# Linear attention followed by a channel mix on one core: a new order table with new engine and PSUM choices

## The chip, the cores and the metric

The kernel runs on one core of one Trainium2 chip. The metric is the device time of one execution in microseconds (us); less is better. The engines that appear below are TensorE (PE, with its weight loads PEld), VectorE (DVE), ScalarE (ACT), GpSimd (POOL) and SyncE (SP, which here only issues transfers). Every engine works through its own instructions in order and waits for others by semaphores. PSUM is the memory into which TensorE writes its results.

## The reference

Two layers follow each other. The first is linear attention over 8 batches, 8 heads, 576 positions and head size 64, the second a channel mix over the 512 joined channels. Cut to what is computed:

```python
def phi(x):                                   # w_phi is 64 x 128
    proj = np.einsum('bhsd,df->bhsf', x, w_phi)
    proj = proj - np.max(np.abs(proj), axis=-1, keepdims=True)
    return np.concatenate([np.exp(proj), np.exp(-proj)], axis=-1)
q_p, k_p = phi(q), phi(k)
kv = np.einsum('bhsf,bhsd->bhfd', k_p, v)
z = np.sum(k_p, axis=2)
attn = np.einsum('bhsf,bhfd->bhsd', q_p, kv) / (np.einsum('bhsf,bhf->bhs', q_p, z)[..., None] + 1e-06)
x = attn.transpose(0, 2, 1, 3).reshape(8, 576, 512)
x_prev = x moved down by one position, zero in front
xk = mu_k * x + (1.0 - mu_k) * x_prev
xr = mu_r * x + (1.0 - mu_r) * x_prev
k = np.maximum(xk @ w_k, 0.0)                 # w_k is 512 x 1024
v = k * k @ w_v                               # w_v is 1024 x 512
out = v / (1.0 + np.exp(-(xr @ w_r)))         # w_r is 512 x 512
```

Inputs and output are float32; the kernel multiplies in bfloat16.

## The kernel before

The attention is cut into 32 pairs of heads, pair n being heads 2a and 2a+1 of batch b with n = 4b + a. The channel mix is cut into 8 batches, and two neighbouring batches share one more tile of 128 positions, the edge tile `e0` to `e3`. Every piece of work is an `op` with a name, an engine and a function that issues its instructions. The names, with the line of `kernel.py` that their instructions carry in the profile:

For the pairs (number n behind the name): `pt` transposes k and q on TensorE (L338), `pa` and `pb` copy the two halves of it out of PSUM; from batch 2 on `tr` does the same by a transposing transfer on SP's queue (L352). `kp` and `qp` project k and q (L566), `rk` and `rq` take the maxima (VectorE reductions, L579 and L584), `em` and `ea`, `eb` are the exponentials for k on ScalarE (L591, L605), `va` and `vb` scale v by a factor from `em` (L597). `mh`, `mt`, `mc` bring the maxima of q into the layout that `qt`, the projection of q in transposed form, adds (L615, L620, L630); `qa` and `qb` are the exponentials for q (L643). `kv` multiplies k's features with v (L656), `kc` copies the product, `nd` forms numerator and denominator (L677), `ra` and `rd` divide (L685, L689). Then the result is transposed: for pairs 0 to 7 by `xt` on TensorE and the copies `xe`, `xf` (L715), for the others by the transposing transfer `xz` on SP's queue (L700) and the small copy `xu` (L706). `df` is the difference to the position before (L726), and `xa` and `xb` mix with `mu_k` and `mu_r` (VectorE, L732).

The last 64 positions of the pairs of one batch are done together by small operations whose names carry the batch: `tp`, `rt`, `mhe`, `mte`, `mce`, `eme`, `ekt`, `qte`, `eqe` (batch 0 has three such groups, `0.0`, `0.1`, `0.2`).

For the channel mix (batch and part behind the name): `h` multiplies with `w_k` (eight parts, L810), `rl` is the rectification (L206 on ScalarE, L208 on VectorE), `sq` the square (L212 on ScalarE, L214 on VectorE or GpSimd), `r` multiplies with `w_r` (four parts, L829), `th` is a hyperbolic tangent that gives the sigmoid (L835), `v` multiplies with `w_v` (four parts, L843), `ob` joins them (VectorE, L849) and `so` stores on SP's queue (L856). `rle`, `sqe`, `he`, `re`, `ve` belong to the edge tiles.

Loads: `hk` and `hq` bring the first pair in float32, `lk0.0.d` and `lq0.0.d` cast it; `lk` and `lq` load k and q of a batch (GpSimd's queue, L321), `lv` loads v (two halves `.0` and `.2` of each batch; GpSimd's or SP's queue, L327), `wk`, `wr`, `wv` the weights in two parts each (GpSimd's queue, L432). A load issued by GpSimd stands in the same order as its computations.

No loop decides the order. One string, `ORDER`, lists all 1498 names, and the kernel calls them in that order; what an engine executes is that list with the other engines' entries left out. Behind a name stand the choices: `/ENG` is the engine where there is one to choose, `:i` the PSUM tile, `+n@i` are n matmuls on constants ahead of the operation, into tile i, that keep TensorE busy. Entries that end in `.d`, and `tr0` to `tr31`, issue nothing, except the two casts.

```python
    def order(self):
        self.place = {}
        out = []
        for word in ORDER.split():
            name, _, n = word.partition("+")
            name, _, on = name.partition("/")
            name, _, i = name.partition(":")
            out.append(self.ops[name])
            out[-1]["on"] = on
            out[-1]["fill"] = tuple(map(int, n.split("@"))) if n else None
            for (tag, key) in out[-1]["alloc"]:
                if tag in ("P", "mo"):
                    self.place[key] = int(i)
```

PSUM has two tiles of one bank, M0 and M1, for `pt`, `xt`, `mt`, `mte`, `qte` and all channel-mix products, and three of two banks, P0 to P2, for the projections (`tp` among them), `qt`, `kv` and `nd`. An operation that takes a tile waits until its last reader is done. Buffers in SBUF are few as well, and a later use waits for the earlier one: `BUFS` gives 2 for k's features (`kpn`), for q's (`qpn`) and for the differences `d`, 3 for the rectified parts (`krelu`) and for v (`vt`), 4 for the outputs (`ob`).

The code that issues the work is the same before and after; the functions that the change reaches through the table follow.

Of the kernel before, what the change touches and what calls it, by code (L numbers as in the profile page):

```python
# [31 lines left out]
eb3 pt6.1:0 pt7.0:1 va2/POOL pb6/DVE tr6 qt2:2 pa7/ACT ra1 rd1 mte0.2:0 qa2 lk2.0 lk2.0.d pt7.1:1
mce0.2/DVE qp5:0 pb7/DVE tr7 qte0.2:0 lq2.0 lq2.0.d qb2 rq5 tp1.0:1 xt0:1 va3/POOL eqe0.2 kv2:2
rt1.0 xf0/ACT xe0/ACT kp4:0 mh4/POOL mt3:0 kc2/ACT rk4 xt1:1 df0/POOL mc3/ACT ekt1.0 nd2:2 ra2 ea4
vb3/POOL xe1/DVE qt3:1+1@0 rd2 mt4:0 xf1/ACT mc4/ACT df1/DVE qa3 xt2:1 xa0 kv3:2 eb4 mhe1.0/DVE
xe2/DVE mte1.0:0+1@0 xb0 kc3/ACT kp5:0 qb3 qt4:2 xa1 eme1.0 xf2/DVE nd3:1 rk5 mce1.0/ACT df2/POOL
qa4 ra3 qb4 rd3 lv1.2/POOL lv1.2.d ea5 xa2 xt3:0+7@1 qp6:2 xb1 qte1.0:1 xe3/ACT qp7:1 eb5 xf3/DVE
df3/DVE xa3 em4 qt5:0+1@0 eqe1.0 rq6 vb4/POOL h0.0:0 qa5 va4/POOL rq7 kp6:2 qb5 h0.1:1 rk6 mh6/POOL
kp7:1 rl0.1/ACT kv4:0 va5/POOL rl0.0/ACT tr2.0 tr2.0.d tr8 tr9 mt6:1 kc4/DVE ea6 h0.2:0 rk7 vb5/POOL
eb6 xb2 kv5:0+1@2 mc6/ACT sq0.0/ACT xb3 nd4:2 tr2.2 tr2.2.d tr10 tr11 em6 ea7 h0.3:1 kc5/DVE  # L40
vb6/POOL ra4 rd4 nd5:0 eb7 vb7/POOL rl0.3/DVE qt6:2 rl0.2/ACT ra5 qp8:1 rd5 qa6 lv2.0/SP lv2.0.d
sq0.1/POOL r0.0:1 rq8 qb6 va6/POOL qp9:0 h0.4:0 rq9 th0.0 sq0.3/POOL sq0.2/ACT qt7:2 kv6:1 rl0.4/DVE
qa7 lk3.0 lk3.0.d tp2.0:0 kc6/DVE h0.5:1 mh8/POOL rt2.0 qb7 va7/POOL xt4:0 rl0.5/ACT kp8:1 xf4/DVE
# [973 lines left out]
```

## Time and profile before

| what | value |
|---|---|
| runs | 280.14, 289.3, 278.56 us; median 280.14 |
| profiled execution, span | 275.3 us, granted TensorE clock 1.00 in every stretch |
| profiled execution, own time beside the span | not recorded |
| TensorE | 261.7 us busy in 3682 matmuls |
| VectorE | 234.6 us busy in 388 instructions |
| ScalarE | 223.1 us busy in 413 instructions |
| GpSimd | 142.4 us busy in 193 instructions |
| transfers | 42.89 MB in 65817 packets, 156 GB/s over the span |

The span runs from the first to the last record of one execution; the runs' times lie some microseconds above it. "Busy" counts instructions that compute; a transfer's issue is not counted, though it occupies the engine that issues it. In a list of groups the columns are the line, the engine, the operation with output and input, the count, busy time and mean ns of one instruction, then the idle time ahead of the group's instructions and what ended most of it. In a table by stretch each row gives the length of the stretch, the busy time of each engine with the count of instructions, the granted clock, and the share and rate of the transfers.

Times of some operations in this execution, as they are used below: `kp0` starts at 7.01 us, `ea0` at 8.84, the first channel-mix matmul `h0.0` at 39.6, `h1.0` at 78.4, `va12` at 83.0, `h2.0` at 113.4, `h4.0` at 170.8, `h5.0` at 190.6, `va28` at 203.3, `h6.0` at 226.5, `h7.0` at 248.8 and `v7.0` at 258.3; the matmuls end at 271.05 and the last store at 275.3. `lq0.1` is issued at 2.15 and `wk.1` at 12.2.

### The profile page before, as it was taken

What the parts mean: (1) busy time and instruction counts of PE and PEld (TensorE: products, weight loads), DVE (VectorE), ACT (ScalarE), POOL (GpSimd) and SP (SyncE); (2) the same over time, 40 slices, a digit from 0 to 9 for tenths busy, and PEclk for the clock granted to TensorE, in tenths of its full rate; (3) what the DMA queues carried; (4) which work ended last, traced back from release to release, by engine and by line L of the source; (5) the groups of instructions that cost most, each with busy time, mean ns of one, the idle gap of its engine ahead of it and who ended that gap; (6) DMA issues with size and microseconds to landing.
All of it is one profiled execution on the core that took longest, in us unless ns stands there. A gap on an engine that the chain in (4) does not pass through costs nothing.

```text
span 275.3 us, 8865 instructions
## 1 busy us (share of the span) xinstructions
PE 261.7 (95%) x3682; PEld 154.1 (56%) x3730; DVE 234.6 (85%) x388; ACT 223.1 (81%) x413; POOL 142.4 (52%) x193
## 2 busy tenths in 40 slices
PE   7899889999899999999999999999999999999993
PEld 3567656566555566555565666555566565444542
DVE  6999999999799989999999889998889897864222
ACT  3899999999899997899898999789987777616330
POOL 5799557976818682633459465821931611300200
PEclk9999999999999999999999999999999999999999
DMA  7999999599999899759699998981725324142134
GB/s 147 285 209 250 209 213 174 114 235 175 238 129 200 202 219 185 155 127 248 99 166 164 215 249 142 171 255 41 161 89 88 77 52 100 42 110 67 29 88 116
DMA packets 65817, 42.89 MB, mean 156 GB/s; under 512 B 47152, under 2 KB 57008, under 8 KB 65776
## 3 DMA queue, kind: packets, MB, share of 16 engines
q1 hardware_dynamic: 54496, 27.54, 49.3%
q0 software_dynamic: 11056, 14.42, 29.1%
q8 instruction: 29, 0.48, 0.8%
q10 hardware_dynamic: 224, 0.36, 0.5%
q14 instruction: 12, 0.10, 0.1%
HBM read 33.62 MB, written 9.44 MB: 156 GB/s over the span
## 4 chain that ended last, share of the span: by engine, by line
PE 75%; DVE 8%; ACT 6%; issue 4%; DMA 3%; POOL 2%; SPq 0%; POOLq 0%; ACTq 0%
PE ps_h L810 19%; PE ps_v L843 17%; PE ps_r L829 9%; PE ps_nd L677 5%; PE ps_kv L656 5%; DMA qkT<-nat 3%; PE ps_he L897 3%; PE ps_ve L929 3%; PE ps_k L566 2%; PE ps_qT L630 2%; PE ps_q L566 2%; PE ps_qT L636 2%; ACT k L605 2%; DVE nmk L579 2%; PE ps_f L292 1%
## 5 line engine op out<-in xcount | busy, mean ns | idle before, releaser
L597 POOL TENSOR_TENSOR v<-vt,v 128x576 bf16<-128x576 f32 x59 | 69.8, 1203 | 33.5 <-ACT v L591 31.1
L605 ACT ACTIVATE k<-ps_k 128x1024 bf16<-128x1024 f32 x64 | 64.8, 1047 | 1.3 <-DVE nmk L579 1.3
L643 ACT ACTIVATE q<-ps_qT 128x1024 bf16<-128x1024 f32 x64 | 63.8, 1054 | 1.8 <-PE ps_qT L636 1.7
L810 PE MATMUL ps_h<-xk,wk_bf 128*128 128x512 bf16 x235 | 60.5, 380 | 1.2
L843 PE MATMUL ps_v<-wv_bf,kk 128*128 128x512 bf16 x244 | 58.2, 379 | 0.6
L579 DVE TENSOR_REDUCE nmk<-ps_k 128x8 f32<-128x1024 f32 x32 | 38.8, 1217 | 1.8 <-PE ps_k L566 1.5
L584 DVE TENSOR_REDUCE nmq<-ps_q 128x8 f32<-128x1024 f32 x32 | 38.3, 1217 | 1.6 <-PE ps_q L566 1.4
L843 PEld LDWEIGHTS <-kk 128*128 128x128 bf16 x256 | 24.1, 98 | 27.3
L810 PEld LDWEIGHTS <-wk_bf 128*128 128x128 bf16 x256 | 22.7, 97 | 25.0 <-issue 0.7
L206 ACT ACTIVATE krelu<-ps_h 128x512 bf16<-128x512 f32 x48 | 28.8, 611 | 9.3 <-PE ps_h L810 9.3
L726 POOL TENSOR_TENSOR diff<-xs 128x576 bf16<-128x576 bf16 x15 | 20.2, 1346 | 28.8 <-ACT xs L706 12.7
L214 POOL TENSOR_TENSOR kk<-krelu 128x512 bf16<-128x512 bf16 x18 | 19.1, 1068 | 30.3 <-ACT krelu L206 26.6
L849 DVE SCALAR_TENSOR_TENSOR ob<-rt,ps_v 128x512 f32<-128x512 bf16 x32 | 21.7, 682 | 14.3 <-PE ps_v L843 12.7
L829 PE MATMUL ps_r<-wr_bf,xr 128*128 128x512 bf16 x116 | 31.1, 380 | 0.7
L835 ACT ACTIVATE rt<-ps_r 128x512 bf16<-128x512 f32 x32 | 19.7, 615 | 8.8 <-PE ps_r L829 8.7
L732 DVE SCALAR_TENSOR_TENSOR xk<-diff,mu_k_t,xs 128x576 bf16<-128x576 bf16 x32 | 26.7, 839 | 0.1
L689 DVE TENSOR_TENSOR x_sc<-ps_nd,rden 128x640 bf16<-128x640 f32 x32 | 26.0, 817 | 0.6
L732 DVE SCALAR_TENSOR_TENSOR xr<-diff,mu_r_t,xs 128x576 bf16<-128x576 bf16 x32 | 25.6, 806 | 0.1
L656 PE MATMUL ps_kv<-v,k 64*128 64x65 bf16 x1024 | 22.4, 190 | 0.5 <-ACT q L643 0.2
L566 PEld LDWEIGHTS <-qkT 64*128 64x128 bf16 x512 | 16.5, 94 | 11.0 <-issue 8.0
L656 PEld LDWEIGHTS <-k 64*128 64x128 bf16 x1024 | 19.3, 94 | 5.7 <-issue 1.8
L677 PE MATMUL ps_nd<-kv,q 128*128 128x65 bf16 x512 | 21.4, 193 | 0.0
(102 smaller groups left out, 414.3 us busy)
## 6 DMA issues: line engine op xcount, KB each, us to landing
out_dram<-ob SPq DMA_DIRECT2D x70, 128.0 KB, 2.5
vt<-in_v_dram SPq DMA_DIRECT2D x11, 576.0 KB, 6.1
nat<-in_k_dram POOLq DMA_DIRECT2D x6, 576.0 KB, 7.8
nat<-in_q_dram POOLq DMA_DIRECT2D x6, 576.0 KB, 8.0
vt<-in_v_dram POOLq DMA_DIRECT2D x4, 576.0 KB, 6.0
wk_bf<-in_moe_w_k_dram POOLq DMA_DIRECT2D x2, 512.0 KB, 11.4
wv_bf<-in_moe_w_v_dram POOLq DMA_DIRECT2D x2, 512.0 KB, 10.6
nat<-in_k_dram POOLq DMA_DIRECT2D x3, 288.0 KB, 6.9
```

Of the source, the lines that this page charges most:

```text
L206: nc.scalar.activation(out_, in_, AF.Relu, scale=HALF)
L579: nc.vector.tensor_reduce(t[:, j, :], s["k"].rearrange("p a (g f) -> p (a g) f", f=128), axis=AX.X, op=ALU.max, apply_absolute_value=True, ...
L584: nc.vector.tensor_reduce(t[:, j, :], s["q"].rearrange("p a (g f) -> p (a g) f", f=128), axis=AX.X, op=ALU.max, apply_absolute_value=True, ...
L597: (nc.vector if eng == "DVE" else nc.gpsimd).tensor_tensor(vb[:, a, pn, :, 0:64], vt[b, a // 2][:, a % 2, :].rearrange("p (s d) -> p s d", ...
L605: nc.scalar.activation(s[f"k{pn}"], s["k"].rearrange("p a (g f) -> p (a g) f", f=128), AF.Exp, scale=(1.0 if pn == 0 else -1.0))
L643: nc.scalar.activation(t.rearrange("f x (a p) -> f x a p", a=2), s["qT"].rearrange("f a (x p) -> f x a p", p=64), AF.Exp, scale=(1.0 if pn ...
L656: nc.tensor.matmul(ps[:, hh, pn * 65:(pn + 1) * 65], lhsT=s[f"k{pn}"][r, c, :], rhs=vb[r, a, pn, 2 * g + par, :], start=(pn == 0 and c == ...
L677: nc.tensor.matmul(ps[:, bk, o * 65:(o + 1) * 65], lhsT=tail if sl < 2 else s[f"q{pn}"][:, 2 * G + h, :], rhs=s["kv"][:, h, pn, :], start= ...
L732: nc.vector.scalar_tensor_tensor(out=t[:, a, (b % 2) * S:(b % 2 + 1) * S], in0=s["d"], scalar=mu[:, a:a + 1], in1=xs[:, a, 0:S], op0=ALU.m ...
L810: nc.tensor.matmul(ps, lhsT=wk_bf[:, c, fc * 128:(fc + 1) * 128], rhs=xkt[bp][:, c, m0:m0 + 512], start=(c == 0), stop=(c == NDC - 1))
L829: nc.tensor.matmul(ps, lhsT=xrt[bp][:, c, m0 + ci * 128:m0 + (ci + 1) * 128], rhs=wr_bf[:, c, :], start=(c == 0), stop=(c == NDC - 1))
L843: nc.tensor.matmul(ps, lhsT=s["kk"][:, fc, ci * 128:(ci + 1) * 128], rhs=wv_bf[:, fc, :], start=(fc == 0), stop=(fc == NFC - 1))
```

## The change

Only the string `ORDER` is rewritten. The same 1498 names stand in it, with the same matmuls on constants. 148 entries have another engine, 151 another PSUM tile, and a large part stand at another place. The engine choices that differ, by kind (from, to, count):

| kind | changes |
|---|---|
| `sq` | ACT to POOL 14, DVE to POOL 7, DVE to ACT 5, POOL to DVE 4, POOL to ACT 2, ACT to DVE 1 |
| `sqe` | DVE to POOL 4, ACT to DVE 2 |
| `rl`, `rle` | ACT to DVE 13, DVE to ACT 12 |
| `df` | DVE to POOL 9, POOL to DVE 3 |
| `xu` | ACT to POOL 7, ACT to DVE 3, POOL to DVE 2, POOL to ACT 2, DVE to POOL 1 |
| `va`, `vb` | POOL to DVE 6, DVE to POOL 2 |
| `lv` (issue) | SP to POOL 6, POOL to SP 2 |
| `kc` | DVE to ACT 5, ACT to DVE 4 |
| `mc`, `mce` | ACT to DVE 7, DVE to ACT 5 |
| `mh`, `mhe` | DVE to POOL 4, POOL to DVE 4 |
| `pa`, `pb`, `xe`, `xf` | DVE to ACT 6, ACT to DVE 4 |
| casts of the first pair | k: DVE to ACT, q: ACT to DVE |

At the start, `pt1.1` moves ahead of `tp0.0` and `kp0`, and most of GpSimd's load issues stand in one row behind `kp1`. The first part of the table:

```diff
--- before.py
+++ after.py
-ones hk hq ident dve2 hk.d hq.d wphi wphi.d lk0.1 lk0.1.d lq0.1 lq0.1.d mus mus.d lk0.2 lk0.2.d dve3
-lq0.2 lq0.2.d lv0.0/POOL lv0.0.d lk0.0.d/DVE lq0.0.d/ACT lv0.1/SP lv0.1.d pt0.0:0+9@0 lv0.2/SP
-lv0.2.d pt0.1:1 pa0/DVE pb0/ACT tr0 dve1 tp0.0:0+1@2 kp0:1 rt0.0 qp0:2 rk0 eme0.0 mhe0.0/POOL ekt0.0
-pt1.0:1+1@0 lk1.0 lk1.0.d pa1/ACT mte0.0:0 rq0 ea0 lq1.0 lq1.0.d pt1.1:1+2@2 pb1/DVE tr1 lk1.2
-lk1.2.d eb0 kp1:2+2@2 tp0.1:0 lq1.2 lq1.2.d rt0.1 em0 rk1 qp1:1+1@1 ekt0.1 mh0/POOL eme0.1 wk.0
-wk.0.d mt0:1+1@1 mc0/ACT mce0.0/DVE rq1 ea1 qt0:0+1@2 wk.1 wk.1.d wk.d pt2.0:1 qa0 pt2.1:0
...
+hk wphi mus wphi.d mus.d ident lk0.1 lq0.1 lk0.1.d lq0.1.d hq ones dve2 dve3 hk.d hq.d lk0.0.d/ACT
+lq0.0.d/DVE pt0.0:1+9@0 pa0/DVE pt0.1:0 pt1.1:1+2@2 pb0/ACT tr0 dve1 tp0.0:0+1@2 rt0.0 kp0:1
+pt1.0:0+1@0 qp0:2 rk0 pb1/ACT ekt0.0 pa1/ACT eme0.0 ea0 em0 eb0 tr1 rq0 kp1:2+2@2 tp0.1:0 rt0.1
+lk0.2 lq0.2 lk1.0 lv0.1/POOL lq1.0 lk1.2 wk.0 mh0/POOL lq1.2 lv0.0/SP lv0.0.d mhe0.0/POOL vb0/POOL
+lv0.2/POOL lk0.2.d lq0.2.d mt0:1+1@1 pt2.0:0 mc0/ACT qp1:1+1@1 ekt0.1 eme0.1 pa2/ACT qt0:0+1@2
```

Up to the first channel-mix matmul, and into the stretch behind it (`xb0` ahead of `rd2`; `sq0.0` on POOL):

```diff
-eb3 pt6.1:0 pt7.0:1 va2/POOL pb6/DVE tr6 qt2:2 pa7/ACT ra1 rd1 mte0.2:0 qa2 lk2.0 lk2.0.d pt7.1:1
...
-vb3/POOL xe1/DVE qt3:1+1@0 rd2 mt4:0 xf1/ACT mc4/ACT df1/DVE qa3 xt2:1 xa0 kv3:2 eb4 mhe1.0/DVE
-xe2/DVE mte1.0:0+1@0 xb0 kc3/ACT kp5:0 qb3 qt4:2 xa1 eme1.0 xf2/DVE nd3:1 rk5 mce1.0/ACT df2/POOL
...
-eb6 xb2 kv5:0+1@2 mc6/ACT sq0.0/ACT xb3 nd4:2 tr2.2 tr2.2.d tr10 tr11 em6 ea7 h0.3:1 kc5/DVE
-vb6/POOL ra4 rd4 nd5:0 eb7 vb7/POOL rl0.3/DVE qt6:2 rl0.2/ACT ra5 qp8:1 rd5 qa6 lv2.0/SP lv2.0.d
-sq0.1/POOL r0.0:1 rq8 qb6 va6/POOL qp9:0 h0.4:0 rq9 th0.0 sq0.3/POOL sq0.2/ACT qt7:2 kv6:1 rl0.4/DVE
...
-kp9:0 h0.6:1 rk9 lv2.2/POOL lv2.2.d eb8 kv7:2 th0.2 df4/DVE qp11:1 sq0.5/DVE rl0.6/ACT h0.7:0 xa4
...
+ea3 pb5/ACT tr5 pt6.1:1 eb3 pb6/ACT qt2:2 qa2 pt7.1:0 lk2.0 mhe0.2/POOL lq2.0 va2/POOL va3/POOL
+vb2/POOL wk.1 vb3/POOL lv1.0.d qp5:0 mte0.2:1 tr6 mce0.2/ACT pb7/DVE rq5 tr7 wv.1.d wv.0.d wv.d qb2
...
+xt1:1 mt3:0 nd2:2 xf1/ACT mc3/ACT ea4 mt4:0 kv3:1 mc4/ACT kc3/ACT qt3:1+1@0 eb4 xe1/DVE ra2 df0/POOL
+xb0 rd2 wr.0 df1/POOL xa0 xb1 wr.1 xt2:1 kp5:0 qt4:2 lk2.0.d wk.1.d wk.d lq2.0.d qa3 qb3 eme1.0
...
+df2/POOL vb4/POOL va5/POOL vb5/POOL va4/POOL lv1.2/POOL xa2 xe3/DVE xf3/DVE mce1.0/DVE df3/DVE xa3
+qp7:1 qp6:2 qte1.0:1 qt5:0+1@0 rq6 h0.0:0 rq7 wr.1.d wr.0.d wr.d lv1.2.d eqe1.0 qa5 rl0.0/ACT qb5
+kp6:2 h0.1:1 rk6 kv4:1 kc4/DVE xb2 rl0.1/ACT mh6/POOL sq0.0/POOL sq0.1/POOL kv5:0+1@2 ea6 eb6 tr2.0
+tr2.0.d tr8 tr9 kc5/DVE kp7:1 mt6:1 h0.3:0 nd5:0 nd4:2 rk7 rl0.3/ACT ea7 em6 eb7 sq0.3/POOL
+lv2.0/POOL vb6/POOL lk3.0 va6/POOL h0.2:0 rl0.2/ACT tr2.2 tr2.2.d mc6/DVE xb3 ra5 ra4 rd4 rd5 r0.0:1
...
+vb7/POOL sq0.4/POOL lk4.0 mh8/POOL lv2.2/POOL lq3.0.d lv2.0.d rk8 ekt2.0 th0.1 ea8 eme2.0 eb8 r0.2:0
...
+sq0.5/POOL v0.1:0 vb9/POOL va9/POOL df4/POOL mh10/POOL df5/POOL rk11 ob0.1 xb4 xa4 xa5 eqe2.0
...
+xt7:1 tp3.0:0 kv10:2 xt6:0 kp12:1 kc10/ACT xf6/ACT xf7/ACT rt3.0 qt10:2 xe6/DVE rk12 xe7/DVE
+mhe3.0/DVE ekt3.0 r0.3:0 nd9:0 v0.3:1 lk5.0 df6/POOL df7/POOL vb11/POOL xa6 ra9 rd9 xa7 lq4.0.d qa10
```

Behind that, the entries of SP's queue (`xz`, `so`), the loads of v and `va16`:

```diff
-kp12:2 xf7/ACT xf6/DVE qt10:1 xe6/DVE ekt3.0 xz8 xz8.d xe7/DVE r0.3:0 df6/DVE qa10 rk12 df7/POOL
...
-h1.5:1 rk15 sq1.4/POOL eb14 lv4.0/SP lv4.0.d r1.2:0 lk5.0 lk5.0.d xz11 xz11.d rl1.5/DVE ea15 qp16:2
...
-rle0.1/ACT kp16:2 vb14/POOL qp17:0 qa14 so1.0 so1.0.d v1.1:1 rq17 va14/POOL qb14 xz12 xz12.d rk16
...
-xa11 eme4.0 ve0:0 em16 ra15 ob1.3 qa16 va16/POOL so1.2 so1.2.d rd15 qb16 h2.0:1 va17/POOL obe0 xz14
...
-h5.3:1 mh28/POOL sq5.1/ACT lv7.2/POOL lv7.2.d rq30 eme7.0 v4.1:0 kc26/ACT vb27/POOL ea28 rl5.3/DVE
-vb29/DVE rl5.4/ACT xb22 nd27:0 rl5.5/ACT h5.6:1 ra26 eb29 sq5.4/DVE rd26 h5.7:0 df24/DVE xz26 xz26.d
...
+eqe3.0 r1.0:1 rq12 rq13 so0.1 so0.0 so0.2 xz8 lv3.0/SP xz8.d em12 th1.0 r1.1:0 qp14:1 h1.2:1 nd11:0
...
+ob1.0 xz12 xz11 xz11.d so1.0 lv4.2/POOL lq5.0.d ekt4.0 qp17:1 qt14:2 kp16:0 rq17 rk16 so0.0.d xz12.d
...
+mc16/DVE r1.3:1 vb15/POOL df10/POOL lv4.0/POOL va15/POOL sqe0.0/POOL sqe0.1/POOL kc14/ACT ra13 rd13
...
+vb16/POOL vb17/POOL obe0 tr5.0 tr5.2 so1.2 xz13 xz13.d lv5.0/SP so1.3 soe0 xz14 xz15 so1.1 va16/DVE
...
+ra27 mc28/DVE nd26:1 h5.5:0 rd27 sq5.4/DVE ra26 rd26 so4.1 xz25 soe1 xz25.d ea29 em28 vb29/DVE
+rl5.5/ACT eb29 h5.6:1 h5.7:0 va29/POOL so4.2 lv7.2/SP xz27 so4.0 sq5.5/POOL rl5.6/ACT rl5.7/ACT
...
+vb30/DVE ra28 rd28 xa25 mt30:0 kv30:0 mc30/ACT th5.3 kc30/ACT kv31:2 qt30:1 so5.1 xz26 xz26.d
```

`lv5.2` is issued by SP in the old table and by POOL in the new one.

## The prediction

> **What bounds the kernel now.** The page's table of engines comes first. It names no single limit: TensorE is busy nearly all the time, VectorE and ScalarE over four fifths of it, and only GpSimd (POOL) is half idle.
>
> ```profile
> PE 261.7 (95%) x3682; PEld 154.1 (56%) x3730; DVE 234.6 (85%) x388; ACT 223.1 (81%) x413; POOL 142.4 (52%) x193
> ```
>
> An average over 275.3 us hides stages with different limits, so the second view is busy time by stretch. I cut at 39.6 (the first MoE matmul, `h0.0`), 83.0 (`va12`) and 203.0 (`va28`), and 271.0, where the matmuls end.
>
> ```profile
> core 0: us, PE busy (x) PEld busy (x) DVE busy (x) ACT busy (x) POOL busy (x), PEclk, DMA share, GB/s
> 0.00:39.60 39.60, 34.48 (x557) 22.32 (x560) 35.49 (x76) 33.92 (x75) 28.81 (x50) 1.00 1.12 224
> 39.60:83.00 43.40, 41.09 (x737) 25.48 (x746) 41.64 (x66) 41.67 (x74) 30.58 (x36) 1.00 0.99 176
> 83.00:203.00 120.00, 118.53 (x1763) 69.65 (x1787) 111.48 (x168) 109.14 (x200) 70.84 (x95) 1.00 0.89 174
> 203.00:271.00 68.00, 67.58 (x636) 36.63 (x640) 45.55 (x80) 38.34 (x68) 12.13 (x14) 1.00 0.35 76
> ```
>
> Up to 39.6 the vector engines set the pace: TensorE idles 5.1 us. From 39.6 to 83 VectorE and ScalarE are each 96% busy and TensorE still idles 2.3 us. After 83 TensorE is the limit, idle 1.5 us of 120 and 0.4 of 68. So an order can win at most the idle 5.1 + 2.3 + 1.5 + 0.4 = 9.3 us, and it can lose without limit.
>
> The third view, the chain that ended last, agrees: TensorE holds three quarters of it.
>
> ```profile
> PE 75%; DVE 8%; ACT 6%; issue 4%; DMA 3%; POOL 2%; SPq 0%; POOLq 0%; ACTq 0%
> ```
>
> The fourth is the list of POOL's waits. It is idle because it works in order and what it needs is late; two of the entries name the VectorE mixes of line 732.
>
> ```profile
> POOL v L597 <- ACT v L591: 31.1, 11, 9.3
> POOL kk L214 <- ACT krelu L206: 26.6, 4, 15.3
> POOL diff L726 <- DVE xr L732: 5.5, 2, 3.7
> POOL v L597 <- DVE xk L732: 2.2, 1, 2.2
> ```
>
> The fifth is the order of time around 166 us. While VectorE's `xk` runs (166.02 to 166.83), POOL's `diff` takes 1.74 us against 1.28 in most of its runs, about the 0.59 they share.
>
> ```profile
> 166.02 0.81 DVE L732 SCALAR_TENSOR_TENSOR xk<-diff,mu_k_t,xs 128x576 bf16<-128x576 bf16 x1
> 166.24 1.74 POOL L726 TENSOR_TENSOR diff<-xs 128x576 bf16<-128x576 bf16 x1 [2.41 <-PE ps_qT L636]
> ```
>
> Over the whole timeline, 39 of the 64 reductions at lines 579 and 584 lie for more than 60% of their length beside a POOL computation, and 3 of the 64 mixes at line 732 do; the 22 squares on VectorE never do. So VectorE operations with two SBUF inputs (mixes, `df`, `sq`, `va`) and POOL computations take turns, and their times add.
>
> The Trainium skill (SBUF — State Buffer, Who interferes with whom) says the same more strictly: the pair of ports that VectorE and GpSimd share is "an exclusive lock", the loser of the race waits for the whole instruction, and a VectorE operation with two SBUF inputs takes part only against a GpSimd operation that reads SBUF. The row above shows both running for part of the time in the records. By the rule, which lets nothing overlap, the middle stretch below comes to +1.0 at least; by the rows, which leave room for overlap, it may be as low as -1.4. The rule speaks against this change.
>
> **The change part by part.** No operation is added or removed, the warm-up matmuls included. 148 operations and load issues change engine and 151 change PSUM tile. TensorE's own order moves little: before `h0.0`, `h1.0`, `h2.0`, `h4.0`, `h5.0` and `v7.0` stands the same matmul work. So TensorE's 261.7 us stay, and the sum is about its idle time.
>
> *Start, 0 to 39.6.* `pt1.1` (transposes of pair 1) is moved ahead of `tp0.0` and `kp0`. It needs both loads of pair 1; `lq0.1` is issued at 2.15 and the page gives such a load 5.4 us, so it lands at about 7.55. Behind `pt1.1` on TensorE wait `tp0.0` (6.94 now) and `kp0` (7.01), and for these the first reductions and the first exponentials. Four transposes (0.2 to 0.3 us) and two fills later `kp0` starts at about 8.0, 1.0 later. ScalarE also gets `pb1` (0.59) ahead of `ea0`, which goes from 8.84 to about 10.0. From there to the end of `qb3` its queue took 25.6 us without a pause; the new table adds `pa2` 0.69, `mce0.0` and `mce0.2` 0.30 each, `pb6` 0.59, `mc2` 0.28, and takes out `pa7` 0.69 and `xe0` 0.71: +0.8. So `qb3` ends at 10.0 + 25.6 + 0.8 = 36.4 against 34.5. `nd3` follows 0.5 later, `ra3` and `rd3` end at 38.0 (36.8 now), and `xa2`, `xe3`, `xf3`, `mce1.0`, `df3`, `xa3` (0.73 + 0.45 + 0.18 + 0.22 + 0.46 + 0.81) bring `h0.0` to 40.9 at best. VectorE walked in the same way gives 41.4, because `xb0` now stands before `rd2`. I take 41.2: **+1.6**. Bounds: 0 if `lq0.1` lands over 1 us earlier and the queues have room, +2.5 if VectorE's walk holds (+1.8) and `df0`, whose queue on POOL has one load issue more ahead of it (0.77), is late by nearly that. `wk.1` stays under this: issued at about 28 instead of 12.2, it lands 12.4 us later as it does now, at about 40.7.
>
> *39.6 to 83.* POOL receives three squares (`sq0.0`, `sq0.2`, `sq0.5`: 3 x 1.04), two differences (`df4`, `df6`: 2 x 1.28), one `mh` (0.50) and the issue of `lv2.0` (0.77), and gives away two `mhe` (0.94): +6.0. ScalarE loses 1.4 and VectorE 1.1. Now POOL's 30.6 and VectorE's two-input work in this stretch (mixes 7.81, `df` 0.90, `sq` 0.42, together 9.1) make 39.7 of 43.4 us; afterwards 36.6 and 7.8 make 44.4. That is 1.0 over the stretch before any wait for a producer. If the 3.7 us that are free today are such waits and all remain, it is 4.7 over. If POOL's issues of loads (4.7 us) run beside the mixes, it fits, and the 1.4 us taken from ScalarE become a gain. What waits behind a late POOL is `kv` (it needs `va` and `vb`) and the `mix` behind `df`. Between -1.4 and +4.7 I take **+2.5**, nearer the upper row because both partners queue in order.
>
> *83 to 203.* POOL receives 12 squares and loses 2 (+10.4), two `sqe` (+2.1, as squares), one difference net (+1.3), one `xu` net (+0.3), two load issues net (+1.5: `lv4.0`, `lv4.2` and `lv5.2` come from SP's queue, `lv7.2` goes there) and loses one `va` net (-1.2): +14.4. ScalarE loses 4.8, VectorE 3.0, which TensorE can turn into 1.5 at most. POOL with the two-input work (mixes 23.8, `va` 2.3, `df` 3.2, `sq` 3.8: 33.0) goes from 103.8 to 117.5 of 120 us, 87% to 98%. The nearest row for so full a pair is the stretch before: at 39.7 of 43.4, 91%, TensorE lost 5.3%, against 1.2% here. Those 4.1% over 120 us are 4.9; VectorE and ScalarE were fuller there too, so I take half, **+2.5**, between -1.5 and +8.
>
> *After 203.* TensorE is 99% busy and POOL has 56 us free; POOL gains 3, VectorE 3, ScalarE loses 4. Cost nothing, covered by TensorE's own queue; without that cover, 3. The last stores leave in the same order: 0. PSUM tiles: matmuls on one tile stand as far apart as before (median 1.4 us of matmul work for the two single-bank tiles), so 0; a tile that is not yet free would cost one eviction, 0.6 to 0.8, each time.
>
> *SP's queue.* Stores now stand before `xz8` and `xz26`, `xz12` before `xz11`. Some transpositions (`xz9`, `xz11`, `xz22`, `xz29`) would land 2 to 6 us after their readers start today; the readers are moved back too, and what they feed (`h2.0` 113.4, `h5.0` 190.6, `h7.0` 248.8) comes 4.6 us or more after these landings. The tight one is `xz26`, issued behind `so5.1` (ready about 219.6): it lands at 223 to 225, and its copy, difference and mix must follow before `h6.0`, 226.5 today. Price 0, at worst 2.
>
> Sum: 275.3 + 1.6 + 2.5 + 2.5 = 281.9 us of span. No own time of the profiled execution is shown; the runs have 278.56, 280.14 and 289.3, so 4.8 us lie around the span at the median. Forecast 281.9 + 4.8 = **286.7**, 2.3% over 280.14. Two per cent, 5.6 us, is about what a measurement of this kernel can tell from no change.
>
> **The rivals.**
> *Within 2%, 281.7.* The load on POOL is absorbed because its new squares fall into its idle time (`kk` waited 26.6 us for `krelu`, in four waits). Then only the start stays: 275.3 + 1.6 + 4.8. For: after 83 TensorE has MoE matmuls to go on with. Against: three engines then run over 90% at once.
> *Faster, 273.5.* ScalarE and VectorE, both 96% busy from 39.6 to 83, are relieved, the start costs nothing, and TensorE gets back 6.6 of its 9.3 idle us. It decides if the pair stays under its 43.4 us. Against: 36.6 + 7.8 is over that.
> *Far slower, 294.* `lv4.0` is issued behind `df10` (104.9 now) instead of at 92.5; at its 8.8 us to landing it comes at about 115, while `va16`, now on VectorE, could start at 112.3, and the whole VectorE queue waits behind it. One such wait costs 2.8; four of this kind beyond the sum, 7 to 11 us.
>
> **How the numbers follow.** Forecast 0.42, far slower 0.08, within 2% 0.35, faster 0.15. So slower 0.50, same 0.35, faster 0.15. The likeliest case alone spans 285.8 to 291. The range reaches into the others: down to 276.5 (start 0, middle -1.4, late -1.5, with 4.1 around it), up to 295 (start 2.5, middle 4.7, late 8, with 4.5 around it).
>
> **What would show it.** `h0.0` at about 41.2 and `kp0` near 8.0 prove the start; POOL above 36 us busy between `h0.0` and `va12`, with `kv` waiting for POOL or TensorE idle over 2.3 us there, proves the middle; TensorE idle above 1.5 us in the stretch from `va12` to `va28`, with POOL 85 busy, proves the late part. `h0.0` at 39.6 or earlier, or TensorE idle shrinking after it, makes the forecast wrong.

## The result and the profile after

The changed kernel takes 303.51 us (median of 4 runs, 302.5 to 306.45) against 281.66 for the kernel before: ratio 1.091, 95% interval 1.079 to 1.103. It is 21.9 us slower by the medians. (The ratios here and below leave out disturbed runs, above all of the kernel before, so this one is above 303.51 / 281.66 and stands for about 25 us.) The forecast was 286.7, the range 276.5 to 295.0.

The profiled execution of the changed kernel has a span of 304.3 us and an own time of 306.45, so about 2 us lie around a span. The profiled execution of before (275.3) lies at the low end of its kernel's runs and this one at the high end, so the two stand 29 us apart, 7 more than the medians. The sums below are made between these two executions, the comparisons of time between runs.

The table of engines of the page of after:

```profile
PE 269.5 (89%) x3683; PEld 156.0 (51%) x3730; DVE 261.9 (86%) x385; ACT 218.2 (72%) x387; POOL 175.7 (58%) x226
```

GpSimd rose by 33 us, as the change says. (Its busy time contains the load issues that it makes, 31 before and 35 after, contrary to what is said of the columns above.) VectorE has three instructions fewer and is busy 27 us longer, so its instructions took longer. The chain that ended last has moved to it, from 8% to 31%:

```profile
PE 48%; DVE 31%; issue 7%; POOL 4%; DMA 4%; ACT 3%; SPq 1%; DVEq 0%; POOLq 0%
```

Busy time by stretch of after, cut at the same operations as before (`h0.0`, `va12`, `va28`):

```profile
0.00:45.40 45.40, 35.35 (x557) 21.92 (x560) 37.66 (x70) 35.09 (x78) 34.70 (x55) 0.99 1.13 206
45.40:96.00 50.60, 43.92 (x738) 26.48 (x747) 46.79 (x66) 41.10 (x70) 35.14 (x40) 0.94 0.93 168
96.00:233.60 137.60, 126.16 (x1821) 73.22 (x1845) 130.32 (x178) 109.19 (x186) 87.87 (x110) 0.99 0.69 141
233.60:300.20 66.60, 64.06 (x573) 34.37 (x579) 46.73 (x74) 32.81 (x55) 17.95 (x23) 1.00 0.34 80
```

TensorE idles 10.1, 6.7, 11.4 and 2.5 us (first number minus PE), together 30.7 against 9.3. From 96 to 233.6 VectorE is busy 130 of 137.6 us; ScalarE, which was the fullest beside it, now has room.

Which instructions grew is read in the groups of VectorE, here the mixes of line 732, first before, then after (last columns: busy time, mean ns):

```profile
L732 DVE SCALAR_TENSOR_TENSOR xk<-diff,mu_k_t,xs 128x576 bf16<-128x576 bf16 x32 | 26.7, 839 | 0.1
L732 DVE SCALAR_TENSOR_TENSOR xr<-diff,mu_r_t,xs 128x576 bf16<-128x576 bf16 x32 | 25.6, 806 | 0.1
```

```profile
L732 DVE SCALAR_TENSOR_TENSOR xk<-diff,mu_k_t,xs 128x576 bf16<-128x576 bf16 x32 | 35.6, 1124 | 0.3 <-POOL diff L726 0.2
L732 DVE SCALAR_TENSOR_TENSOR xr<-diff,mu_r_t,xs 128x576 bf16<-128x576 bf16 x32 | 30.9, 974 | 0.8 <-POOL diff L726 0.8
```

Same work, 14 us more. In order of time, the longest one (`xa17`) of after:

```profile
173.03 1.16 POOL L597 TENSOR_TENSOR v<-vt,v 128x576 bf16<-128x576 f32 x1
173.52 3.51 DVE L732 SCALAR_TENSOR_TENSOR xk<-diff,mu_k_t,xs 128x576 bf16<-128x576 bf16 x1
174.15 1.03 POOL L214 TENSOR_TENSOR kk<-krelu 128x512 bf16<-128x512 bf16 x1
175.15 1.26 POOL L726 TENSOR_TENSOR diff<-xs 128x576 bf16<-128x576 bf16 x1
```

The mix started 0.49 us after a GpSimd scaling. It came to an end only at 177.03, 0.62 after the third GpSimd computation in a row: 2.7 us longer than its usual 0.81. The small cast of line 480 (`mhe3.0`, 0.17 us undisturbed) shows the same:

```profile
83.59 2.52 POOL L726 TENSOR_TENSOR diff<-xs 128x576 bf16<-128x576 bf16 x2
84.31 2.95 DVE L480 CAST mhlt<-me 128x4 bf16<-128x4 f32 x1
86.06 1.17 POOL L597 TENSOR_TENSOR v<-vt,v 128x576 bf16<-128x576 f32 x1
```

I call the excess over the undisturbed duration "stretch". I took it for every VectorE operation with inputs in SBUF (mixes, `df`, `sq`, `va`, `vb`, `xu`, `mh`, `mhe`), as its time from start to end minus 0.81 for `xa`, 0.78 for `xb`, 0.45, 0.42, 0.75, 0.75, 0.17, 0.37 and 0.36, and counted those over 0.15. Before: 3 of 120 operations, 1.4 us. After: 32 of 113, 29.9 us. Laid beside the time lost, cut at operations that do not change engine:

| stretch of the kernel | before us | after us | longer | VectorE's stretch in after |
|---|---|---|---|---|
| start to `h0.0` | 39.6 | 45.4 | 5.8 | 3.2 |
| `h0.0` to `h1.0` | 38.8 | 44.8 | 6.0 | 5.7 |
| `h1.0` to `h2.0` | 35.0 | 39.5 | 4.5 | 5.0 |
| `h2.0` to `h4.0` | 57.4 | 65.0 | 7.6 | 8.1 |
| `h4.0` to `h6.0` | 55.7 | 59.1 | 3.4 | 6.0 |
| `h6.0` to the last store's issue | 45.4 | 47.3 | 1.9 | 2.0 |

The two columns agree outside the first and the fifth row. That is a correlation; the cause is left to the experiments.

### The profile page after: what moved, and what is told of

Same layout as the page of the kernel before. It is cut to its first block, busy times and chain, and to the rows that moved or that the text cites. A ratio compares the mean times of both kernels' runs of the same rounds, so it can differ in the third digit from the quotient of the medians.

```text
span 304.3 us, 8862 instructions
## 1 busy us (share of the span) xinstructions
PE 269.5 (89%) x3683; PEld 156.0 (51%) x3730; DVE 261.9 (86%) x385; ACT 218.2 (72%) x387; POOL 175.7 (58%) x226
## 4 chain that ended last, share of the span: by engine, by line
PE 48%; DVE 31%; issue 7%; POOL 4%; DMA 4%; ACT 3%; SPq 1%; DVEq 0%; POOLq 0%
PE ps_v L843 12%; PE ps_h L810 11%; PE ps_r L829 7%; DVE xk L732 5%; DVE nmq L584 4%; DMA vt<-in_v_dram 4%; PE ps_kv L656 3%; DVE nmk L579 3%; DVE x_sc L689 3%; PE ps_nd L677 2%; DVE xr L732 2%; DVE krelu L208 2%; DVE ob L849 2%; PE ps_k L566 2%; PE ps_qT L630 2%
## 5 line engine op out<-in xcount | busy, mean ns | idle before, releaser
L597 POOL TENSOR_TENSOR v<-vt,v 128x576 bf16<-128x576 f32 x55 | 68.5, 1260 | 33.4 <-ACT v L591 29.5
L643 ACT ACTIVATE q<-ps_qT 128x1024 bf16<-128x1024 f32 x64 | 63.1, 1036 | 7.1 <-PE ps_qT L636 7.0
L810 PE MATMUL ps_h<-xk,wk_bf 128*128 128x512 bf16 x239 | 62.8, 388 | 3.2 <-DVE ob L849 1.7
L214 POOL TENSOR_TENSOR kk<-krelu 128x512 bf16<-128x512 bf16 x33 | 35.2, 1073 | 32.4 <-ACT krelu L206 30.6
L206 ACT ACTIVATE krelu<-ps_h 128x512 bf16<-128x512 f32 x47 | 28.1, 603 | 16.3 <-PE ps_h L810 16.1
L810 PEld LDWEIGHTS <-wk_bf 128*128 128x128 bf16 x256 | 23.5, 99 | 29.5 <-issue 6.7
L726 POOL TENSOR_TENSOR diff<-xs 128x576 bf16<-128x576 bf16 x21 | 28.8, 1373 | 12.5 <-DVE xr L732 4.9
L732 DVE SCALAR_TENSOR_TENSOR xk<-diff,mu_k_t,xs 128x576 bf16<-128x576 bf16 x32 | 35.6, 1124 | 0.3 <-POOL diff L726 0.2
L849 DVE SCALAR_TENSOR_TENSOR ob<-rt,ps_v 128x512 f32<-128x512 bf16 x32 | 21.7, 679 | 12.7 <-PE ps_v L843 9.2
L732 DVE SCALAR_TENSOR_TENSOR xr<-diff,mu_r_t,xs 128x576 bf16<-128x576 bf16 x32 | 30.9, 974 | 0.8 <-POOL diff L726 0.8
```

What stands on the lines that cost most here:

```text
L214: (nc.vector if eng == "DVE" else nc.gpsimd).tensor_tensor(out_, in_, in_, op=ALU.mult)
L597: (nc.vector if eng == "DVE" else nc.gpsimd).tensor_tensor(vb[:, a, pn, :, 0:64], vt[b, a // 2][:, a % 2, :].rearrange("p (s d) -> p s d", ...
L643: nc.scalar.activation(t.rearrange("f x (a p) -> f x a p", a=2), s["qT"].rearrange("f a (x p) -> f x a p", p=64), AF.Exp, scale=(1.0 if pn ...
L732: nc.vector.scalar_tensor_tensor(out=t[:, a, (b % 2) * S:(b % 2 + 1) * S], in0=s["d"], scalar=mu[:, a:a + 1], in1=xs[:, a, 0:S], op0=ALU.m ...
L810: nc.tensor.matmul(ps, lhsT=wk_bf[:, c, fc * 128:(fc + 1) * 128], rhs=xkt[bp][:, c, m0:m0 + 512], start=(c == 0), stop=(c == NDC - 1))
```

## The experiments

Theory A: GpSimd computations hold up VectorE where the two meet, VectorE is full, and so the collisions set the time. Theory B: the new order and its start cost the time by waits for producers, and the stretch is incidental.

**A dose in the kernel before.** Fifteen useless GpSimd operations behind the 15 `df` on GpSimd, once with reads of SBUF, once without.

```diff
+ if n in DOSE:                      # the 15 pairs whose df runs on GpSimd
+     op("dm" + N, "POOL", 1.3, 0, lambda: nc.gpsimd.tensor_tensor(dscr, xs[:, a, 64:64 + S], xs[:, a, 0:S], op=ALU.subtract), mixed_in)
```

> The kernel before, with one useless GpSimd difference of 128x576 (1.28 us, the form of df, into a tile that nobody reads) behind each of the 15 df that run on GpSimd: 19 us more on an engine that is half idle. Theory A (GpSimd computations that read SBUF hold up VectorE, and VectorE's queue sets the pace): 4 to 10 of the 15 meet a mix; the stretch of VectorE's operations, 1.4 us in the kernel before, becomes 5 to 12 us and the time rises by 4 to 11 us. Rival (idle time of GpSimd is free): the time stays within 1% (2.8 us).

```diff
+     op("dm" + N, "POOL", 1.3, 0, lambda: [nc.gpsimd.memset(dscr, 0.0) for _ in range(2)], mixed_in)
```

> The same 15 places, but with two GpSimd memsets of 128x576 (estimated at 0.58 us each from the 205 ns of the 128x128 memset and the 100 ns of the 128x1) in place of the difference: the same occupation of GpSimd, nothing read from SBUF. If it is the reading that holds VectorE, the mixes keep 0.81 us and the time lies within 1% of the kernel before, and below that of the run with reads by its stretch. If any GpSimd work holds VectorE, stretch and time equal those of the run with reads.

With reads 286.26 us, ratio 1.028 (1.019 to 1.037) to the kernel before; with memsets 280.19, ratio 1.003 (1.000 to 1.006). The same place in both, `xa14`, in order of time, first the run with reads, then the one with memsets:

```profile
136.71 1.28 POOL L789 TENSOR_TENSOR dscr<-xs 128x576 bf16<-128x576 bf16 x1
136.91 1.69 DVE L732 SCALAR_TENSOR_TENSOR xk<-diff,mu_k_t,xs 128x576 bf16<-128x576 bf16 x1
```

```profile
132.76 1.22 POOL L789 MEMSET dscr<- 128x576 bf16 x2
132.98 0.81 DVE L732 SCALAR_TENSOR_TENSOR xk<-diff,mu_k_t,xs 128x576 bf16<-128x576 bf16 x1
```

The mix loses 0.88 us beside the read and nothing beside two memsets. Over the whole kernel the stretch is 14.4 us with reads, 8.5 of it on operations that met an added read, and 5.0 with memsets (there, but for 0.2 on one `mh`, beside the kernel's own GpSimd work, moved in time). So 19 us more on a half idle engine, whose results nobody awaits, cost 6.1 us over the control. Theory A holds in size and direction; the stretch of 14.4 was above the expected 5 to 12.

**The changed kernel without GpSimd's reads.** Engines, order, tiles and GpSimd's occupation stay; each GpSimd square, scaling and difference becomes a one-column product, which keeps the wait for the inputs, and two memsets. So this kernel leaves those results out.

```diff
+    def wonly(out_, o2, o1, i1, i2=None):
+        [nc.gpsimd.tensor_tensor(o1, i1, i1 if i2 is None else i2, op=ALU.mult)] + [nc.gpsimd.memset(o, 0.5) for o in (out_, o2)]
...
-            (nc.vector if eng == "DVE" else nc.gpsimd).tensor_tensor(out_, in_, in_, op=ALU.mult)
+            nc.vector.tensor_tensor(out_, in_, in_, op=ALU.mult) if eng == "DVE" else wonly(out_, out_[:, 0:288], out_[:, 0:1], in_[:, 0:1])
```

> The changed kernel, with every GpSimd square, scaling of v (va, vb) and difference (df) replaced by one tiny GpSimd product of one column (it keeps the wait for the inputs) and two memsets that last about as long as the computation did. The squares, scalings and differences on GpSimd are left out; table, engines, tiles, waits and GpSimd's occupation stay. Theory A (GpSimd's reads of SBUF hold VectorE): the stretch falls from 29.9 to under 5 us and the time from 303.5 to 277 to 287 us. Theory B (order, start, late producers): the time stays at 297 us or more.

> The control: the same replacement of squares, va, vb and df on GpSimd in the kernel before, with these computations left out. Its stretch is 1.4 us only, so by theory A the time stays within 1% of the kernel before, 277 to 284 us. If the replacement by itself makes a kernel faster (shorter occupation of GpSimd, other waits), this run is faster by over 1.5%, and what the replacement gains in the changed kernel must be reduced by that.

> The same replacement in the changed kernel for the 37 squares on GpSimd alone; these squares are left out. Theory A: about 12 of the 29.9 us of stretch have a square as partner; stretch 14 to 22 us, time 290 to 297 us. Theory B: 300 us or more.

The changed kernel goes from 303.51 to 285.54 us (ratio to the kernel before 1.022, 1.015 to 1.030). The control goes to 282.18 (1.011, 1.005 to 1.017), so the replacement by itself gains nothing. The engines and the mixes of the changed kernel without reads:

```profile
PE 264.7 (93%) x3683; PEld 154.6 (54%) x3730; DVE 234.2 (82%) x385; ACT 217.0 (76%) x387; POOL 172.0 (60%) x452
```

```profile
L732 DVE SCALAR_TENSOR_TENSOR xr<-diff,mu_r_t,xs 128x576 bf16<-128x576 bf16 x32 | 25.5, 808 | 0.6 <-POOL diff L222 0.6
L732 DVE SCALAR_TENSOR_TENSOR xk<-diff,mu_k_t,xs 128x576 bf16<-128x576 bf16 x32 | 25.5, 808 | 1.7 <-POOL diff L222 1.6
```

GpSimd is as busy as in the changed kernel (172.0 against 175.7), VectorE is back at 234.2, and no operation is stretched (one by 0.15 us). Of the medians' 21.9 us 18.0 are gone; by the ratios the loss falls from 9.1% to 2.2%, and the control stands at 1.1%. This shows theory A for the bulk. The run takes away both sides of a meeting: GpSimd's own computations, counted in the same way, were stretched as well, by 11.4 us in the changed kernel against 3.7 before. What this side cost through late results was not separated from VectorE's.

A rival is TensorE's clock, lower in the changed kernel, or raised by constants in place of data. At one clock the differences stay: of the runs with a granted clock of 0.992 to 0.995, 19 of the kernel before took 279.6 to 283.0 us, two of the changed kernel 302.5 and 302.7, three of it without reads 285.3 to 287.3, and five of the control 280.1 to 282.1.

With the squares alone replaced the median was 301.13 us (runs from 296.68 to 301.52; 1.069, 1.052 to 1.086) with 22.3 us of stretch left in the profiled one: scalings and differences make most of the collisions, and of the expected 290 to 297 us only one run of four came in.

**Six small operations.** Not every microsecond of stretch is one of time. Here six entries of the changed kernel get another engine, each listed at the time at which it ran (the entries alone are shown):

```diff
-mhe2.0/DVE mhe3.0/DVE mhe7.0/DVE mh16/DVE mh20/DVE xu8/DVE
+mhe2.0/POOL mhe3.0/POOL mhe7.0/POOL mh16/POOL mh20/POOL xu8/ACT
```

> The changed kernel with six small operations off VectorE, at the times at which they ran: mhe2.0, mhe3.0, mhe7.0, mh16 and mh20 on GpSimd, xu8 on ScalarE. Together they are 2.1 us of VectorE work that took 11.1 us, 9.0 of it stretch. Theory A: VectorE's stretch falls from 29.9 to about 21 us and the time by 5 to 9 us, to 295 to 299. Theory B (order and start): less than 2 us.

303.64 us (1.091, 1.078 to 1.103), no change; the expected 295 to 299 was missed. The trace shows the matmuls of `h1.0` 4.1 us earlier (86.1 against 90.2), but those of `h2.0` no earlier (130.3 against 130.2): `xa10` alone, beside three GpSimd computations, was now stretched by 3.5 us in place of 2.0. A collision taken away moves the two queues against each other, and later ones appear. In all 24.2 us of stretch were left.

**The start.** Two attempts to give the start back, then the second without GpSimd's reads.

```diff
-pt0.1:0 pt1.1:1+2@2 pb0/ACT tr0 dve1 tp0.0:0+1@2 rt0.0 kp0:1 pt1.0:0+1@0 qp0:2 rk0 pb1/ACT ekt0.0 pa1/ACT eme0.0 ea0 em0
+pt0.1:0 pb0/ACT tr0 dve1 tp0.0:0+1@2 rt0.0 kp0:1 qp0:2 rk0 ekt0.0 eme0.0 pt1.0:0+1@0 ea0 pt1.1:1+2@2 pa1/ACT pb1/ACT em0
```

> The changed kernel, with the transposes pt1.1 and the copies behind them back after tp0.0, kp0, qp0, and the first exponentials. The prediction's step on the start: kp0 from 8.3 back to about 7.1 us, ea0 from 10.4 to 9.0, and h0.0 from 45.4 to about 43.5; the end 1 to 2 us earlier (about 302). Rival (VectorE's collisions set the pace from 30 us on): kp0 and ea0 as said, but h0.0 moves by less than 0.7 and the end by less than 1 us.

> The changed kernel with pt1.1 back behind the first exponentials, lv0.0 on GpSimd's queue, lv0.1 and lv0.2 on SP's, and GpSimd's queue up to vb1 in the old order. In the changed kernel lv0.0 lands at 14.5 in place of 12.2 and va1 starts at 22.4 in place of 17.5, behind five load issues. If that row of loads is what the start lost beyond the collisions, kv0 goes from 20.9 to about 19, qb3 from 36.6 to 34.5, h0.0 from 45.4 to 42 to 43, and the end is 2 to 3.5 us earlier. Rival (collisions at xb0, xa2, df3 and xa3 hold h0.0, 3.2 us): h0.0 stays above 44.

> The run with memsets in place of GpSimd's squares, scalings and differences (285.5 us; those computations are left out), and in it the start undone: pt1.1 behind the first exponentials, the three first loads of v and GpSimd's queue up to vb1 as in the old table. If the 3.4 us that remain against the control (282.2) are the start, the time is 281 to 284 and h0.0 at 41 to 42.5 in place of 44.0. Rival (the start is absorbed later, the remainder lies between h0.0 and re0): 285 us or more.

Moving `pt1.1` back brings `kp0` to 6.5 and `ea0` to 8.3, but `qb3` still starts at 36.5 (36.6 in the changed kernel) and `h0.0` at 44.9: 304.0 us. With the loads and GpSimd's queue as before as well, `h0.0` comes at 44.3: 304.99 us. Without GpSimd's reads, 286.84 us against 285.54 with the new start: nothing gained. There ScalarE starts `ea0` at 8.8, as in the kernel before, but needs 29.0 us from there to the end of `qb3`, against 25.6. The copies that it got (`pa1`, `pb1`, `pa2`, `pb6`, `mce0.0`, `mce0.2`, `mc2`, less `pa7` and `xe0`) add 2.2 us; its busy time, overlaps counted once, grows by 1.6 us and its waits by 1.8, most of all ahead of `mce0.0`, `eqe0.2` and `mc1`. So `qb3` ends 3.3 us later than in the kernel before, and `h0.0` comes 3.9 later. That ScalarE's queue is what makes the first matmul of the channel mix late is read from these times; that `pt1.1` is not, is shown by the runs.

**Each half alone.** Old engines in the new order and new engines in the old order, and only the 48 computations that were moved to GpSimd given back. In the first form of two of them the entries stood where GpSimd's entries stand in the table, far ahead of their time for another engine; they were run again with every changed entry listed at its moment in the trace.

```diff
-rl0.1/ACT mh6/POOL sq0.0/POOL sq0.1/POOL
+rl0.1/ACT mh6/POOL sq0.0/ACT sq0.1/POOL
```

> The new order and the new PSUM tiles with all 148 engine choices of the old table. Theory A (collisions): in the changed kernel 32 VectorE operations with SBUF inputs are stretched by 29.9 us in all, because a GpSimd computation runs when they start; 22.7 of these involve an operation whose engine changed. With the old engines at most some 10 to 14 us of stretch stay, the mean of xk falls from 1.12 to below 0.95 us, and the time is 285 to 293 us. Theory B (order): the start, the loads and the positions cost the time whoever does the work; 298 us or more, with mixes still above 1.0.

> The old order and the old PSUM tiles with all 148 engine choices of the new table. Theory A (collisions): GpSimd carries 33 us more in an order in which its work was clear of VectorE's mixes; 10 to 25 us of stretch appear, mixes at 0.95 to 1.1 us, time 288 to 298 us. Theory B (order): without the new order the engine choices alone are worth within 2% of the kernel before, 276 to 286 us.

> The changed kernel, with only those 48 computations given back to VectorE or ScalarE that the change moved to GpSimd (26 squares and edge squares among them). Theory A (collisions): 20.6 us of the 29.9 us of stretch had such a partner or were on such an operation; VectorE and ScalarE get back some 14 us of work, so the stretch falls below 14 us and the time to 287 to 295 us. Theory B (order): 299 us or more.

> All 148 engine choices of the old table in the new order, each changed entry listed at the moment at which it started in the changed kernel's trace. If the 346 us of the run with the old engines in the new order came from entries that stood too early in the queue of another engine, this run is at 285 to 300 us. Rival (new order and old engines don't go together in any case): 320 us or more.

> The changed kernel with the 48 computations that it moved to GpSimd given back to VectorE or ScalarE, and now each listed at the moment at which it started in the changed kernel's trace, so that its new engine does not wait for it too early. Theory (collisions): stretch below 15 us and 287 to 296 us. Rival (the positions belong to the engine choices; VectorE and ScalarE are too full to take the work back): 300 us or more.

And three of these tables without GpSimd's reads:

> The new engine choices in the old order (304.2 us, stretch 20.4 us), with memsets in place of GpSimd's squares, scalings and differences, which are left out. If collisions are what this half of the change costs as well, the stretch goes under 2 us and the time to 281 to 288 us. Rival (other waits of the new engines in the old order): 295 us or more.

> The old engine choices in the new order, each listed at its time (311.2 us, stretch 16.3 us), with the same replacement; GpSimd's squares, scalings and differences are left out. If collisions are most of it: 286 to 296 us. Rival (the positions stall the old engines): 300 us or more; with 16.3 us of stretch to lose, some 295 us would leave 13 us to the positions.

> The changed kernel with 48 computations given back to VectorE and ScalarE (309.2 us, stretch 21.7 us), with the same replacement of what GpSimd still computes; that is left out. If collisions are most of it: 284 to 292 us. Rival (VectorE and ScalarE are too full): 300 us or more.

| order | engines | time us | stretch us | without GpSimd's reads us |
|---|---|---|---|---|
| old | old | 281.7 | 1.4 | 282.2 (1.011) |
| old | new | 304.2 (1.095, 1.076 to 1.115) | 20.4 | 294.1 (1.046) |
| new | old, positions as they stood | 346.1 (1.251, 1.245 to 1.256) | 14.8 | not tried |
| new | old, listed in time | 311.2 (1.107, 1.094 to 1.120) | 16.3 | 302.5 (1.078) |
| new | 48 back, positions as they stood | 310.6 (1.122, 1.114 to 1.129) | 20.8 | not tried |
| new | 48 back, listed in time | 309.2 (1.105, 1.092 to 1.117) | 21.7 | 294.1 (1.048) |
| new | new | 303.5 (1.091, 1.079 to 1.103) | 29.9 | 285.5 (1.022) |

I had expected the old engines to remove most of the stretch and the time with it; half of the stretch went, and the time rose. Neither half is harmless. In the mixed tables other waits are left when the reads are gone: 294.1 and 302.5 us, each above the range expected of collisions alone. Which waits these are was not looked into. New order and new engines together leave 285.5, close to the control, so they fit each other in nearly everything but the collisions. In the timing of the kernel before only 3 of 120 operations meet; the mixed tables have 22 to 28 meetings, the changed kernel 32.

**The price of a meeting by itself.** Sections behind the end of the kernel before, VectorE repeating one operation beside six GpSimd squares.

```diff
+        section(d_mix, 6, none, 0)
+        section(d_mix, 6, p_sq, 6)
+        section(d_mix, 6, p_ms, 10)
+        section(d_red, 5, p_sq, 6)
+        section(d_cast, 10, p_sq, 6)
```

> The kernel before, with a measurement behind its end: eleven short sections in which VectorE repeats one kind of operation beside a row of six GpSimd squares of 128x512 (1.04 us each), beside ten GpSimd memsets, or alone. Theory A (reads of SBUF by GpSimd hold every VectorE operation that needs the port): mixes 0.81 us alone and beside memsets, and 1.4 us or more, or delayed by whole squares, beside squares; the small cast of 128x4 (line 480 in the kernel) and the small difference (line 481), which showed 2.9 and 0.9 us in the changed kernel, are held in the same way; reductions and copies from PSUM are not (1.2 and about 0.4 us). Rival (only operations with two SBUF inputs are held): the casts, copies and memsets of VectorE keep the time that they have alone.

Rows of single source lines (count: shortest/median/longest ns), in this order: mixes alone; squares alone; mixes and squares side by side; mixes beside memsets; reductions from PSUM beside squares; casts of 128x4 alone; then casts of 128x4, differences of 128x4, copies of 128x63, casts from PSUM and memsets of VectorE, each beside squares:

```profile
L1001 DVE SCALAR_TENSOR_TENSOR wr_bf<-wk_bf,mu_k_t x6: 811/819/819, 273.5 to 277.8; 128x576 bf16<-128x576 bf16 x6
...
L995 POOL TENSOR_TENSOR wv_bf<-wk_bf x6: 1040/1040/1040, 279.4 to 285.0; 128x512 bf16<-128x512 bf16 x6
...
L1001 DVE SCALAR_TENSOR_TENSOR wr_bf<-wk_bf,mu_k_t x6: 817/1476/1477, 286.5 to 293.4; 128x576 bf16<-128x576 bf16 x6
L995 POOL TENSOR_TENSOR wv_bf<-wk_bf x6: 1427/1433/1434, 286.7 to 294.3; 128x512 bf16<-128x512 bf16 x6
...
L1001 DVE SCALAR_TENSOR_TENSOR wr_bf<-wk_bf,mu_k_t x6: 818/819/819, 296.2 to 300.4; 128x576 bf16<-128x576 bf16 x6
...
L1004 DVE TENSOR_REDUCE red<-ps_z x5: 1219/1224/1225, 302.6 to 307.7; 128x8 f32<-128x1024 f32 x5
...
L1007 DVE CAST wr_bf<-mu_k_t x10: 170/170/172, 310.1 to 311.9; 128x4 bf16<-128x4 f32 x10
...
L1007 DVE CAST wr_bf<-mu_k_t x10: 170/528/1015, 312.6 to 317.5; 128x4 bf16<-128x4 f32 x10
L1010 DVE TENSOR_TENSOR wr_bf<-mu_k_t,wr_bf x10: 161/528/1016, 320.0 to 324.8; 128x4 bf16<-128x4 f32 x10
L1013 DVE COPY wr_bf<-wk_bf x10: 178/184/947, 327.2 to 332.1; 128x63 bf16<-128x63 bf16 x10
L1016 DVE CAST wr_bf<-ps_z x8: 691/691/693, 334.9 to 339.9; 128x512 bf16<-128x512 f32 x8
L1019 DVE MEMSET wr_bf<- x10: 59/59/59, 342.3 to 343.4; 128x1 bf16 x10
```

In a row of both, mix and square take 1.48 and 1.43 us in place of 0.82 and 1.04. Casts, copies and differences of a few elements go from 0.17 to as much as 1.0. Reductions and casts from PSUM, and memsets, feel nothing (1.22, 0.69, 0.06, shortest and longest alike), and mixes beside GpSimd memsets neither.

The Trainium skill (SBUF — State Buffer, Who interferes with whom) states that a VectorE operation with two SBUF inputs contends with GpSimd only where GpSimd reads SBUF. The dose and the section with memsets (0.82 us) agree. The same section counts copies and casts among the operations that can contend by another way, in modes that use both ports; the casts and copies from SBUF here do, up to 1.02 us, though no row shows the mode.

## Why the prediction was wrong

*Direction and place of the load* were right: slower; GpSimd 35.1 us busy between `h0.0` and `va12` (36.6 forecast) and 87.9 up to `va28` (85); TensorE idle in both. `kp0` came at 8.3 (8.0 forecast) and `ea0` at 10.4 (10.0).

*The step that failed* is the price of GpSimd's added work in the middle and late stretches, +2.5 and +2.5. They measured +7.2 and +17.3 (from `va12` to `va28`, which starts at 203.3 before and at 233.6 after), and VectorE's stretch in them is 5.7 and 17.0 us. The prediction added the two engines' port times, compared the sum with the length of the stretch (44.4 of 43.4, 117.5 of 120) and priced only what did not fit. But here the two queues, each in its own order, did not fill each other's gaps: they met. After these moves more than every fourth VectorE operation with SBUF inputs (32 of 113) met a GpSimd computation and lost 0.93 us on average (29.9 by 32), although GpSimd's busy time and VectorE's undisturbed two-input work together, 43.0 and 122.1 us, are less than the 50.6 and 137.6 us that the stretches came to. The only row shown of a meeting (166 us) had GpSimd as the loser, which was half idle; in the changed kernel VectorE lost, which was already 93 to 96% busy in these stretches of the kernel before. Without GpSimd's reads the lengths from `h0.0` to `h1.0` and from `h2.0` to `h4.0` are 39.6 and 57.3 us, within 1 us of the kernel before.

*The operations counted* were too few as well: only those with two SBUF inputs. The casts and differences of `mh` and `mhe`, 0.36 us for both, gave 8 us of the stretch; 6.4 of it fell on four (`mhe2.0`, `mhe3.0`, `mh16`, `mh20`) that the change moved to VectorE, and of which the prediction booked only what GpSimd gave away.

*The start*, +1.6, measured +5.8: `h0.0` at 45.4 against 41.2 forecast. By the stretch table 3.2 of it are collisions (`xb0`, `xa2`, `df3`, `xa3`), which the walk left out. Without them `h0.0` comes at 44.0, 4.4 late. The walk's cause, `pt1.1`, was real for `kp0`, but undoing it recovered none of the time.

*The 4.8 us around the span* came from setting the span of one execution beside the time of another. Wherever both are on record for the same execution, 1.7 to 2.2 us lie around it.

*TensorE's 261.7 us stay* was wrong by 7.8: with the same matmuls it is busy 269.5, and its granted clock is 0.94 in the stretch from `h0.0` to `va12`. Two runs of this kernel, at clocks of 0.983 and 0.994, took 306.45 and 302.5 us. At equal clock the gap to the kernel before stays, as the runs above show.

*Of the bounds and rivals*: after 203, cost nothing, was right, the last stretch (from `va28` on) is 1.0 us shorter. The far slower case named a late `lv4.0`; it landed later than forecast (122.2 against 115), but `va16` did not start before 130.8, so it held nothing. `xz26` landed at 251.5, 2.3 us ahead of `h6.0`, and the distance from `v5.0` to `h6.0` grew by 1.8 us, near the 2 that the prediction gave as its worst; without the reads that distance is the old one. The rival "within 2%" rested on free time of GpSimd; the dose shows that this time is not free.

*Open*: the last 3.4 us between 285.5 and the control. The profiled execution without reads is longer than that of before in two places: up to `h0.0` (44.0 against 39.6, ScalarE's fuller queue) and from `h1.0` to `h2.0` (39.4 against 35.0). So in that row of the table above the equal size of loss and stretch proves nothing, though no single wait was found there that explains it. Nor is it known why TensorE's clock was lower.

## What to carry to other kernels

Before moving work to a half idle GpSimd, list the VectorE operations that read SBUF and stand near it in time, and price each meeting at the rest of the GpSimd computation (0.9 us on average here), on the engine that loses; a sum of busy times does not show it. As far as tried here, a mix can stand beside GpSimd work that only writes (0.82 us), and VectorE work that reads PSUM beside GpSimd's squares (1.22 and 0.69 us). An order and its engine choices go together: in this kernel half of one table with half of the other cost as much as the slower of the two or more (304.2 to 346.1 us against 303.5).

## What was not expected of the hardware

A VectorE operation can wait for several GpSimd computations in a row: `xa17` for three (3.51 us), `mhe3.0` for three (its cast 2.95 us), `xa10` of the run with six operations moved for three (4.29 us), while in the section of mixes and squares they took turns one by one. What decides between the two was not tested.

A cast of 128x4 elements, 0.17 us, can cost 2.95 us in this way, more than any mix of 128x576 in the kernel before.
